# A decode-attention kernel with a gated MLP: other sizes and fewer pieces of K_0, V_15 and the output projection, and wq issued as 16 partitions and then 112

## The chip, the cores and the metric

The kernel runs on one core of one Trainium2 chip. The metric is the device time of one execution in microseconds (us), lower is better. A run is one execution; medians are over several runs. The span of a profile is a little shorter than the time of its run (650.4 against 652.2 us here), so spans are compared with spans and times with times.

## The reference

One token (S = 1, D = 512) goes through attention over a cache of 16384 keys in 32 heads of 128, and through a small gated MLP; a scalar gate mixes the two. All inputs are bf16.

```python
def _A_ref(x, k_cache, v_cache, wq, wo):                  # k_cache, v_cache: (1, 32, 16384, 128)
    q = (x @ wq).reshape(B, Sq, H, Dh).transpose(0, 2, 1, 3)   # wq: (512, 4096)
    scores = jnp.einsum('bhqd,bhkd->bhqk', q, k_cache) * Dh ** (-0.5)
    p = softmax(scores, axis=-1)
    o = jnp.einsum('bhqk,bhkd->bhqd', p, v_cache)
    return o.transpose(0, 2, 1, 3).reshape(B, Sq, H * Dh) @ wo  # wo: (4096, 512)

g = sigmoid((x * gate_w).sum(-1, keepdims=True))
return g * _A_ref(x, ...) + (1 - g) * _B_ref(x, ...)      # _B_ref: gated MLP, F = 1792  [cut]
```

The caches are 268 MB of the 279.6 MB read. Almost nothing is written.

## The kernel before

The heads are taken in 16 pairs. The keys of a pair (K_i) and its values (V_i) are 8 MB each, 128 partitions by 64 KB, and are loaded through three buffers of 8 MB in turn. A load waits, on the SyncE (SP) queue that issues it, until the load three places earlier has been used. The buffer that will hold V_0 first holds wq (4 MB), w_in and w_out.

```python
K_CUTS = (0, 128, 256)            # pieces of K_0 and K_15, of 256
V_CUTS = (0, 160, 224, 256)       # pieces of V_15; 32 of them are one tile on TensorE
WO_CUTS = (0, 16, 24, 28, 30, 31, 32)   # pieces of wo, in heads
WIDE = 24                         # heads taken in "wide" groups of 8; the rest one by one
...
sp.op(lambda e: e.dma_start(out=wq, in_=A_wq.rearrange("(p c) n -> p (c n)", c=DC)),
      inc=(ld_q, 16))
sp.op(... w_in ...); sp.op(... w_out ...)
...
for n, kind, i in loads:          # K_0, K_1, V_0, K_2, V_1, ...
    wait = [user[n - 3]] if n >= 3 else [w_free] if buf[n % 3] is setup else []
    ...
    if n == 0:
        cuts, sems = K_CUTS, ld_kf
    elif i == NP - 1:
        cuts, sems = (K_CUTS, ld_kh) if kind == "k" else (V_CUTS, ld_vp)
    ...
for j, (a, b) in enumerate(zip(WO_CUTS[:-1], WO_CUTS[1:])):
    sp.op(... wo[:, a * D:b * D] ..., inc=(ld_o[j], 16))
...
def add(lhsT, rhs, wait, mark=False):     # one head: two matmuls 1 x 256
    ...
for j, (a, b) in enumerate(zip(WO_CUTS[:-1], WO_CUTS[1:])):
    for k in range(max(a, WIDE), b):
        y_ok = add(o2[:, k:k + 1], wo[:, k * D:(k + 1) * D],
                   [(ld_o[j], 16)] if k == a else (), k == H - 1)
    if b == 28:
        add(ones_f[:, 0:1], d_sb[:, :], [w_ok])   # sum of the wide groups, copied by ScalarE
...
for q in (sp, act):
    open_late(nc, q)     # the first load of SP and of ScalarE is issued ahead of the start barrier
```

`k_s` and `v_s`, which tell VectorE (DVE) and TensorE (PE) that data is there, are raised by GpSimd when a load has landed.

The softmax here doesn't subtract the row's maximum and nothing guards it: scores larger than these inputs give would overflow.

## Time and profile before

| | before |
|---|---|
| time, median of the first 6 runs | 651.86 us (651.61 to 652.16) |
| span of the profile | 650.4 us |
| read from memory | 279.58 MB |
| first large DMA packet | 1.0 us |
| wq landed | 12.06 us |
| last load landed | 647.94 us |
| PE's last matmul ended | 648.80 us |

A landing is the time at which a load's data is complete. The landings are read from the trace's records of DMA packets (a packet is one piece that one of the 16 DMA engines moves): each load ends in sixteen semaphore writes of 4 bytes (720 for the 45 loads on the SP queue before), and the last of them is taken.

From the page (the summary that is kept of each profiled execution), the DMA rows (busy tenths of the 16 DMA engines in 40 slices of 16.3 us, and what they moved), the totals, and the row of wq in the table of DMA issues (KB, us from issue to landing):

```profile
span 650.4 us, 7753 instructions
...
DMA  9999999999998999999999999999999999999998
GB/s 382 444 439 451 447 391 451 451 431 407 451 451 387 451 451 447 391 451 451 407 431 451 447 391 451 451 431 407 451 451 395 443 451 447 391 439 463 394 427 341
...
HBM read 279.58 MB, written 0.00 MB: 430 GB/s over the span
...
bufs<-in_A_wq_dram SPq DMA_DIRECT2D x1, 4096.0 KB, 12.4
```

The kernel is bound by DMA from end to end. (The swing between 387 and 451 is only in which slice a long packet is counted. Sixteen packets are in flight at a time, and one of 64 KB takes 2.42 us: spread over their durations, the packets give 433 GB/s all the way.) At that rate 279.58 MB take 645.7 us, so a change can save at most the few microseconds at both ends.

The stretch in which wq arrives, in the view of windows (busy us and number of instructions for each engine, PE clock, DMA share, GB/s):

```profile
core 0: us, PE busy (x) PEld busy (x) DVE busy (x) ACT busy (x) POOL busy (x), PEclk, DMA share, GB/s
1.00:12.00 11.00, 0.61 (x4) 0.34 (x4) 4.56 (x5) 3.04 (x3) 1.95 (x6) 1.00 0.99 399
```

The end of the chain of work that ended last (start us, us, what). L101 are matmuls of the wide groups, L88 repeated matmuls (fillers, there to keep PE busy), L693 the heads taken one by one and the sum of the wide groups:

```profile
643.48 1.01 PE ps_all L101 x8
644.49 0.43 PE ps_all L88
644.92 0.85 PE ps_all L101 x6
645.77 0.43 PE ps_all L88
646.20 0.85 PE ps_all L101 x8
647.05 0.23 PE ps_all L88
647.28 0.42 PE ps_all L693 x8
647.70 0.02 issue
647.73 1.08 PE ps_all L693 x12
648.80 0.02 issue
648.83 0.41 DVE res L708
```

PE ends 0.86 us after the last landing (648.80 and 647.94), so PE and DMA end almost together.

And from the timeline, V_15's copy by ScalarE (ACT) out of PSUM, where PE's results (ps_all) stand; that is the end of V_15's work on PE:

```profile
639.29 0.59 ACT L578 COPY d_sb<-ps_all 128x512 f32<-128x512 f32 x1 [11.74 <-ACTq L84]
```

### The profile page before, as it was taken

To read this page: it belongs to the slowest core of one execution; us is meant where nothing else is said; L and a number is where in the kernel's file an instruction comes from. 1 tells how busy PE (TensorE), PEld (TensorE's weight loads), DVE (VectorE), ACT (ScalarE), POOL (GpSimd) and SP (SyncE) were. 2 spreads that over 40 slices of the span, in tenths; PEclk is the share of its full clock that TensorE was granted. 3 is DMA by queue.
4 is the path that set the end of the run, shared out by engine and by line. 5 is a ranking of instruction groups with operands and counts; after the bars stand their busy time and mean duration, and the time that the engine had idled before them with its cause. 6 is when DMAs were issued, how large, how long until landed. Compare 5 with 4: busy or idle time off the path is not lost. (4 is left out here: it accounts for less than half of the span.)

```text
span 650.4 us, 7753 instructions
## 1 busy us (share of the span) xinstructions
PE 437.8 (67%) x2462; PEld 46.9 (7%) x1320; DVE 336.4 (52%) x159; ACT 45.8 (7%) x112; POOL 2.2 (0%) x10
## 2 busy tenths in 40 slices
PE   0675876847477675857757486584858857488878
PEld 0000010000101000010100101000010100001022
DVE  3487719256280745618156370835628174465600
ACT  2211010100001000010100001000010100001011
POOL 1000000000000000000000000000000000000000
PEclk9868797958889687888958779795887969689888
DMA  9999999999998999999999999999999999999998
GB/s 382 444 439 451 447 391 451 451 431 407 451 451 387 451 451 447 391 451 451 407 431 451 447 391 451 451 431 407 451 451 395 443 451 447 391 439 463 394 427 341
DMA packets 6491, 279.60 MB, mean 430 GB/s; under 512 B 727, under 2 KB 986, under 8 KB 1370
## 3 DMA queue, kind: packets, MB, share of 16 engines
q1 hardware_dynamic: 6482, 279.58, 99.6%
q8 instruction: 1, 0.02, 0.0%
q10 hardware_dynamic: 8, 0.00, 0.0%
HBM read 279.58 MB, written 0.00 MB: 430 GB/s over the span
## 5 line engine op out<-in xcount | busy, mean ns | idle before, releaser
L557 DVE TENSOR_TENSOR bufs<-bufs,qb x64 | 281.5, 4419 | 165.1 <-DVEq L84 165.1
L88 PE MATMUL ps_all<-bufs,ident 128*128 x960 | 272.2, 444 | 0.0
L475 PE MATMUL ps_all<-bufs,ident 128*128 x64 | 28.8, 451 | 143.6 <-PEq L84 143.6
L101 PE MATMUL ps_all<-bufs,p_t 128*8 x1024 | 80.3, 388 | 28.9 <-PEq L84 18.3
L542 DVE TENSOR_REDUCE s_sb<-ps_all 128x64 f32<-128x512 f32 x64 | 44.1, 689 | 100.2 <-DVEq L84 100.2
L88 PE MATMUL ps_all<-zero,ident 128*8 128x512 bf16 (+1 forms) x147 | 57.3, 390 | 0.0
L569 ACT ACTIVATE p_t<-s_sb 64x256 f32 (+1 forms) x32 | 13.3, 415 | 439.7 <-ACTq L84 439.3
L475 PEld LDWEIGHTS ps_all<-bufs,ident 128*128 128x128 bf16 x64 | 6.3, 99 | 367.7 <-issue 367.7
L101 PEld LDWEIGHTS ps_all<-bufs,p_t 128*8 x1024 | 18.4, 82 | 162.3 <-issue 161.5
L510 PE MATMUL ps_all<-pick,d_sb 128*128 128x2 f32 x128 | 17.0, 254 | 14.8 <-PEq L84 14.8
L510 PEld LDWEIGHTS ps_all<-pick,d_sb 128*128 128x128 f32 x128 | 15.7, 193 | 22.9 <-issue 22.9
L578 ACT COPY d_sb<-ps_all 128x512 f32<-128x512 f32 x16 | 9.4, 586 | 103.5 <-ACTq L84 103.5
L583 ACT CAST ps_all<-zero 128x512 f32<-128x512 bf16 x15 | 8.8, 589 | 1.7
L458 PE MATMUL ps_all<-zero,ident 128*128 128x512 bf16 x18 | 7.0, 389 | 0.0
L364 DVE TENSOR_TENSOR bufs<-ps_all,ident 128x896 f32<-128x896 f32 x2 | 2.1, 1086 | 8.3 <-PE ps_all L88 8.3
L647 DVE TENSOR_TENSOR o_sb<-ps_all,rl 128x32 bf16<-128x32 f32 x1 | 0.2, 192 | 11.4 <-PE ps_all L510 11.4
L306 PE MATMUL ps_all<-xgw,const-float32-1.0 1*128 1x3 f32 x2 | 0.6, 360 | 8.0 <-DVE xgw L303 8.0
L569 ACT ACTIVATION_READ_ACCUMULATOR p_t<-s_sb (+1 forms) x32 | 5.9, 185 | 0.0
L644 DVE RECIPROCAL rl<-ps_all 128x32 f32<-128x32 f32 x1 | 0.4, 358 | 10.4 <-PE ps_all L531 10.4
L88 PE MATMUL ps_all<-bufs,xb 128*128 x12 | 4.9, 536 | 0.0
L101 PE MATMUL ps_all<-bufs,u 128*1 x14 | 2.6, 372 | 3.1 <-ACT ps_all L410 2.4
L329 PE MATMUL ps_all<-bufs,xb 128*128 x4 | 2.3, 573 | 3.2 <-DMA bufs<-in_B_w_in_dram 3.2
(76 smaller groups left out, 44.9 us busy)
## 6 DMA issues: line engine op xcount, KB each, us to landing
bufs<-in_A_k_cache_dram SPq DMA_DIRECT2D x4, 4096.0 KB, 33.7
bufs<-in_A_v_cache_dram SPq DMA_DIRECT2D x1, 5120.0 KB, 33.1
bufs<-in_A_wq_dram SPq DMA_DIRECT2D x1, 4096.0 KB, 12.4
bufs<-in_A_v_cache_dram SPq DMA_DIRECT2D x1, 2048.0 KB, 37.6
bufs<-in_A_wo_dram SPq DMA_DIRECT2D x1, 2048.0 KB, 23.6
bufs<-in_B_w_in_dram SPq DMA_DIRECT2D x1, 1792.0 KB, 15.6
bufs<-in_A_v_cache_dram SPq DMA_DIRECT2D x1, 1024.0 KB, 39.6
bufs<-in_A_wo_dram SPq DMA_DIRECT2D x1, 1024.0 KB, 25.7
```

The source lines that it names most:

```text
L88: ins = eng.matmul(out, lhsT=lhsT, rhs=rhs, **flags).ins
L101: ins = eng.matmul(bank[0:m, 0:n], lhsT=lhsT, rhs=rhs, **flags).ins
L329: if n else matmul_on(nc, e, lambda: e.matmul(args[0], lhsT=args[1], rhs=args[2], **flags), [at, (xa, 0)]))
L364: dve.op(lambda e, h=h, zh=zh: e.tensor_tensor(out=zm[:, 2 * h * ZB:2 * (h + 1) * ZB].rearrange("p (b m k) -> p b m k", b=2, k=FhC), in0=z ...
L458: e.matmul(args[0], lhsT=args[1], rhs=args[2], **flags)
L475: matmul_on(nc, e, lambda: e.matmul(s3, lhsT=ident[:, :], rhs=k3[:, :, 0:W], start=True, **flags), [(kw, 0)])
L510: ins = e.matmul(o2, lhsT=d_sb[:, r * Dh:(r + 1) * Dh], rhs=pick[:, r * 2:(r + 1) * 2], start=False, stop=False, skip_group_check=True)
L542: return e.tensor_reduce(out=s_sb[:, c * QK:(c + 1) * QK], in_=s_ps[c % 2].rearrange("p (j w) -> p j w", w=W), axis=AX.X, op=ALU.add)
L557: e.tensor_tensor(out=k3, in0=k3, in1=qi, op=ALU.mult).then_inc(mul_s, 1)
L569: e.activation(out=p_t[rows, bass.ds(at, NG * 8)].rearrange("p (t c) -> p t c", c=8)[:, :, 4 * s:4 * s + 4], in_=s_sb[rows, :].rearrange(" ...
L578: return e.copy(out=d_sb[:, :], in_=d_ps)
L583: e.copy(out=d_ps, in_=zero[:, :]).then_inc(drn_s, 1)
```

## The change

Its intent, as far as the edit shows it, is fewer loads and an earlier first packet: the first load has 16 rows, one for each of the 16 DMA engines, and both loads of wq are issued ahead of the start barrier. The end on PE is cut to fit: two wide groups, and the sum of the wide groups is added first.

```diff
--- before.py
+++ after.py
@@ -36,9 +36,9 @@
 NT = NG // TG
 ZB = F // 4
 K_CUTS = (0, 128, 256)
-V_CUTS = (0, 160, 224, 256)
-WO_CUTS = (0, 16, 24, 28, 30, 31, 32)
-WIDE = 24
+V_CUTS = (0, 192, 256)
+WO_CUTS = (0, 16, 27, 31, 32)
+WIDE = 16
 inv_sqrt_dh = float(Dh) ** -0.5
 
 
@@ -151,7 +151,7 @@
             todo.append(i)
 
 
-def open_late(nc, queue):
+def open_late(nc, queue, loads):
     kind = queue.eng.engine
     blocks = {b.name: b for b in nc.m.functions[0].blocks}
     first = nc.m.functions[0].blocks[0].instructions
@@ -159,10 +159,11 @@
     barrier = [i for i in first[at:] if i.engine == kind][:2]
     assert isinstance(barrier[1], mybir.InstEventSemaphore)
     todo = blocks[queue.name].instructions
-    assert isinstance(todo[0], mybir.InstDMACopy)
     for i in barrier:
         first.remove(i)
-    todo[1:1] = barrier
+    n = next(j for j, i in enumerate(todo) if not isinstance(i, mybir.InstDMACopy))
+    assert n >= loads
+    todo[loads:loads] = barrier
 
 
 def gated_mix_kernel(nc, A_x, A_k_cache, A_v_cache, A_wq, A_wo, B_x, B_w_in, B_w_sp, B_b_sp,
@@ -233,7 +234,6 @@
         sem(n) for n in ("ld_x", "ld_g", "ld_q", "ld_w", "ld_u", "st_out"))
     ld_k = [sem(f"ld_k{b}") for b in range(2)]
     ld_v = [sem(f"ld_v{b}") for b in range(2)]
-    ld_kf = [sem(f"ld_kf{b}") for b in range(len(K_CUTS) - 1)]
     ld_kh = [sem(f"ld_kh{b}") for b in range(len(K_CUTS) - 1)]
     ld_vp = [sem(f"ld_vp{b}") for b in range(len(V_CUTS) - 1)]
     ld_o = [sem(f"ld_o{b}") for b in range(len(WO_CUTS) - 1)]
@@ -273,8 +273,9 @@
     act.op(lambda e: e.dma_start(out=wb_row[:, 0:1], in_=B_w_sp), inc=(ld_g, 16))
     act.op(lambda e: e.dma_start(out=wb_row[:, 1:2], in_=B_b_sp.rearrange("(a d) -> a d", a=1)),
            inc=(ld_g, 16))
-    sp.op(lambda e: e.dma_start(out=wq, in_=A_wq.rearrange("(p c) n -> p (c n)", c=DC)),
-          inc=(ld_q, 16))
+    wq_src = A_wq.rearrange("(p c) n -> p (c n)", c=DC)
+    for a, b in ((0, 16), (16, P)):
+        sp.op(lambda e, a=a, b=b: e.dma_start(out=wq[a:b], in_=wq_src[a:b]), inc=(ld_q, 16))
     sp.op(lambda e: e.dma_start(out=w_in, in_=B_w_in.rearrange("(p c) f -> p (c f)", c=DC)),
           inc=(ld_w, 16))
     sp.op(lambda e: e.dma_start(out=w_out, in_=B_w_out.rearrange("(p k) n -> p (k n)", k=FhC)),
@@ -338,7 +339,7 @@
     z_ok = (pe.sem, pe.n)
     def pe_queries(e):
         e.wait_ge(*g_free)
-        e.wait_ge(ld_q, 16)
+        e.wait_ge(ld_q, 32)
         wq4 = wq.rearrange("p (c n j s d) -> p c n j s d", c=DC, n=4, s=2, d=Dh)
         xa, wa = (counter(e, n, 0) for n in ("xq", "wq"))
         with e.Fori(0, DC) as c:
@@ -608,9 +609,7 @@
         wait = [user[n - 3]] if n >= 3 else [w_free] if buf[n % 3] is setup else []
         src = (k_src if kind == "k" else v_src)[i]
         cuts, sems = (0, KP), [(ld_k if kind == "k" else ld_v)[i % 2]]
-        if n == 0:
-            cuts, sems = K_CUTS, ld_kf
-        elif i == NP - 1:
+        if i == NP - 1:
             cuts, sems = (K_CUTS, ld_kh) if kind == "k" else (V_CUTS, ld_vp)
         for a, b, done in zip(cuts[:-1], cuts[1:], sems):
             sp.op(lambda e, a=a, b=b, n=n, src=src: e.dma_start(
@@ -626,8 +625,7 @@
         e.nop().then_inc(loaded, -16)
 
     def pool_pairs(e):
-        for j in range(len(ld_kf)):
-            hand(e, ld_kf[j], k_s, 1)
+        hand(e, ld_k[0], k_s, 2)
         with e.Fori(0, NP // 2 - 1):
             hand(e, ld_k[1], k_s, 2)
             hand(e, ld_v[0], v_s, NT)
@@ -696,12 +694,11 @@
                 mark=mark and s == NC - 1, inc=(half, 1) if mark and s == 0 else None)
         return ok
 
+    add(ones_f[:, 0:1], d_sb[:, :], [w_ok])
     for j, (a, b) in enumerate(zip(WO_CUTS[:-1], WO_CUTS[1:])):
         for k in range(max(a, WIDE), b):
             y_ok = add(o2[:, k:k + 1], wo[:, k * D:(k + 1) * D],
                        [(ld_o[j], 16)] if k == a else (), k == H - 1)
-        if b == 28:
-            add(ones_f[:, 0:1], d_sb[:, :], [w_ok])
     for q in (dve, act):
         mine = range(NC)[:NC // 2] if q is dve else range(NC)[NC // 2:]
         for s in mine:
@@ -722,8 +719,8 @@
     for q in (sp, pool, act, dve, pe):
         q.issue()
     nc.switch_bb("end")
-    for q in (sp, act):
-        open_late(nc, q)
+    open_late(nc, sp, 2)
+    open_late(nc, act, 1)
 
 
 _INS = ['A_x', 'A_k_cache', 'A_v_cache', 'A_wq', 'A_wo', 'B_x', 'B_w_in', 'B_w_sp', 'B_b_sp', 'B_w_out', 'gate_w']
```

The order of instructions on the engines is otherwise that of before.

## The prediction

> **What bounds the kernel now.** DMA. In the page's 40 slices DMA is busy at nine tenths or more nearly everywhere; 279.58 MB pass in 650.4 us. In the trace's packet records the first large packet starts 1.0 us after the span's start, each engine then moves 32 KB packets back to back in 1.21 us (16 engines: 432 GB/s), and the last load lands at 647.9 us. 279.58 MB at 433 GB/s is 645.7 us: only some 5 us are not streaming, at the start and after the last landing. PE (67%) and DVE (52%) have slack; the DMA issues show 30 to 40 us from issue to landing, so the queue never runs dry.
>
> **The change, part by part.**
>
> 1. K_0 in one piece. By the timeline DVE starts on K_0 at 32.7 us, on its first half; the whole lands at 37.8. DVE starts some 5.5 us later, and K_0's buffer comes free at about 67 instead of 61.1 us. The next load need only be queued before V_0 has landed, at 76.5 us. Nothing on the critical path.
>
> 2. Fewer pieces. Near the end 1 KB packets take 46 ns where 38 would be full rate; a small piece costs about 0.07 us. Three net fewer: -0.2 to -0.3 us.
>
> 3. Tail (timeline from 615 us). PE takes V_15 as 5, 2, 1 tiles, from 631.15 us, 0.6 us after the landing. With 6 and 2 it starts at about 633.6. A tile costs 0.93 us at full clock, 1.28 in the half-clock window seen from 630 to 637 us. So V_15 ends about 641.9 instead of 639.0, and the chain to the output projection moves with it. Then two wide groups instead of three, but PE waits for ACT's 0.59 us copy right after them, and 16 narrow heads at 0.15 us follow instead of 8. PE, no longer the last landing, ends the kernel: about +3 us.
>
> 4. wq as 16 and 112 partitions. Meant to start the first packets sooner; worth at most 0.3 us. [...]
>
> **Prediction.** 651.9 + 3.0 + 2.4 - 0.3 = 657.0 us; 8 in 10 between 653.3 and 662.5. Faster by over 2%: 0.005; within 2%: 0.925; slower by over 2%: 0.07.
>
> **What would show it.** First 16 packets of wq at 2 to 5 us, and wq landing later than 12.1 us: step 4 right. If later ones stay at 1.21 us and wq lands at 12, step 4 is about -0.3 and the time near 654.5. The last load landing while PE is still in V_15 or the wide groups, and a final chain of PE alone: step 3 right. DVE's first multiply near 38 us plus step 4's delay, no DMA gap near 76 us: step 1 right.
>
> **What would make it wrong.** The 112 rows spread so badly that wq takes 20 us more (slower by over 2%)[...].

The sum came to 657.0 us: +3.0 for the tail (step 3), +2.4 for wq (step 4) and -0.3. The +2.4 was the estimate that packets into 16 and into 112 partitions would be slow; the ground given for it is cut, as no trace had shown it, and so is one case of what would make the forecast wrong. The "at most 0.3 us" of step 4 is an estimate too: before, the sixteen first packets start from 1.00 to 1.75 us, at 1.26 us on average.

## The result, and the profile after

| | before | after |
|---|---|---|
| time, median | 651.9 us (20 runs, 651.61 to 652.84) | 662.15 us (10 runs, 660.94 to 663.03) |
| ratio of fast runs | | 1.0156, 95% interval 1.0147 to 1.0165 |
| span of the profile | 650.4 us | 660.6 us |
| wq landed | 12.06 us | 20.64 us |
| last load landed | 647.94 us | 657.04 us |
| PE's last matmul ended | 648.80 us | 659.00 us |

A ratio is the mean time of one kernel's fast runs over that of the other's of the same rounds, so it is not quite the ratio of the medians quoted. By the threshold of 2% the two are "the same"; the difference of 10 us is nonetheless far outside the noise.

The rows of the page that answer to those above:

```profile
span 660.6 us, 7753 instructions
...
DMA  9999999999999999999999999999999999999997
GB/s 222 389 444 436 440 393 444 444 440 436 425 413 444 444 436 440 421 417 444 444 436 433 405 440 444 444 433 436 405 440 444 444 433 433 405 438 450 426 413 306
...
HBM read 279.58 MB, written 0.00 MB: 423 GB/s over the span
...
bufs<-in_A_wq_dram SPq DMA_DIRECT2D x1, 3584.0 KB, 21.3
...
bufs<-in_A_wq_dram SPq DMA_DIRECT2D x1, 512.0 KB, 6.5
```

The first slice moves 222 instead of 382 GB/s, although its DMA digit is still a 9: the engines are busy, with packets that take longer. The windows say the same of the stretch in which wq arrives (it is 19.6 us long now):

```profile
core 0: us, PE busy (x) PEld busy (x) DVE busy (x) ACT busy (x) POOL busy (x), PEclk, DMA share, GB/s
1.00:20.60 19.60, 0.61 (x4) 0.35 (x4) 4.56 (x5) 3.04 (x3) 1.95 (x6) 1.00 1.01 226
```

The end of the chain of work that ended last, and V_15's copy in the timeline (L691 are now the single heads and the sum, L101 the second wide group):

```profile
655.32 0.63 PE ps_all L101 x8
655.95 0.02 issue
655.97 0.59 ACT d_sb L687
656.56 0.04 issue
656.61 2.39 PE ps_all L691 x36
659.00 0.02 issue
659.02 0.41 DVE res L705
```

```profile
650.82 0.58 ACT L579 COPY d_sb<-ps_all 128x512 f32<-128x512 f32 x1 [14.00 <-ACTq L84]
```

So there are two losses. The stream is late by 8.6 us when wq has landed and by 9.1 us at its end, and PE ends 1.96 us instead of 0.86 us after the last landing, another 1.1 us.

The packet records show the first loss in detail. All rows of wq are 32 KB. Sorted by start, sixteen at a time (one per engine), they took on average, in us:

| packets | before | after |
|---|---|---|
| 1 to 16 | 1.89 | 3.62 |
| 17 to 32 | 1.24 | 2.80 |
| 33 to 48 | 1.22 | 2.29 |
| 49 to 64 | 1.21 | 1.79 |
| 65 to 80 | 1.21 | 1.80 |
| 81 to 96 | 1.21 | 2.04 |
| 97 to 112 | 1.21 | 2.27 |
| 113 to 128 | 1.21 | 2.10 |

All 16 engines take part in both kernels: at 3 us sixteen packets are in flight in both traces. 112 rows are seven groups of sixteen packets. The engines do start a little sooner (1.00 to 1.38 us after the change, 1.00 to 1.75 us before), as intended. All later loads run at 1.21 us for 32 KB and 2.42 us for 64 KB, as before.

### The profile page after: what moved, and what is told of

Same layout as the page of the kernel before. It is cut to its first block, busy times and chain, and to the rows that moved or that the text cites. A ratio compares the mean times of both kernels' runs of the same rounds, so it can differ in the third digit from the quotient of the medians.

```text
span 660.6 us, 7753 instructions
## 1 busy us (share of the span) xinstructions
PE 431.5 (65%) x2469; PEld 47.6 (7%) x1328; DVE 336.3 (51%) x159; ACT 45.8 (7%) x112; POOL 2.1 (0%) x10
## 5 line engine op out<-in xcount | busy, mean ns | idle before, releaser
L88 PE MATMUL ps_all<-bufs,ident 128*128 x960 | 267.5, 436 | 0.0
L476 PE MATMUL ps_all<-bufs,ident 128*128 x64 | 28.6, 447 | 148.0 <-PEq L84 148.0
L101 PE MATMUL ps_all<-bufs,p_t 128*8 x1024 | 80.4, 389 | 31.7 <-PEq L84 21.1
L101 PEld LDWEIGHTS ps_all<-bufs,p_t 128*8 x1024 | 18.5, 82 | 164.8 <-issue 164.0
L330 PE MATMUL ps_all<-bufs,xb 128*128 x4 | 2.1, 517 | 4.0 <-DMA bufs<-in_B_w_in_dram 4.0
```

The source lines that it names most:

```text
L88: ins = eng.matmul(out, lhsT=lhsT, rhs=rhs, **flags).ins
L101: ins = eng.matmul(bank[0:m, 0:n], lhsT=lhsT, rhs=rhs, **flags).ins
L330: if n else matmul_on(nc, e, lambda: e.matmul(args[0], lhsT=args[1], rhs=args[2], **flags), [at, (xa, 0)]))
L476: matmul_on(nc, e, lambda: e.matmul(s3, lhsT=ident[:, :], rhs=k3[:, :, 0:W], start=True, **flags), [(kw, 0)])
```

## The experiments

Main theory, at the start: the cost lies in the destination. The packets of a load that covers only some of the partitions of SBUF (the on-chip memory that the loads fill) last longer because of the partitions that they go to, as the first sixteen do after the change (3.62 us against 1.89). The expectations call this the "port theory". Rivals: a second load or the later barrier costs the time; the memory side does (rows read in another order); only odd sizes such as 112 are slow. For the other parts of the change: they cost about 1 us on PE (from the traces), or 2.7 us (the prediction), and K_0 nothing. Twelve kernels were run, four or five runs and one profile of each; each was also checked against the reference.

### 1. wq alone in 16 and 112 partitions

```diff
 kernel before, plus:
-sp.op(... out=wq, in_=A_wq ...)
+for a, b in ((0, 16), (16, P)):
+    sp.op(... out=wq[a:b], in_=wq_src[a:b] ...)
+open_late(nc, sp, 2)
```

> The kernel before with wq alone issued as 16 and 112 partitions (both ahead of the start barrier, as in the change). Port theory: the whole loss at the start comes back, +8.6 to +9.1 us (ratio 1.013 to 1.014), the first 16 packets last 3 to 4 us, wq lands near 20.6 us instead of 12.1. Rival, that the late start of everything else or another part of the change costs the time: under +1 us, wq lands by 12.5 us.

Measured: 661.27 us against 651.77, ratio 1.0144 (1.0128 to 1.0159), that is +9.4 us. wq landed at 20.74 us, and its packets took 3.56, 2.81, 2.26, 1.82, 1.77, 2.03, 2.25 and 2.09 us, the pattern of the changed kernel. This part alone makes over nine tenths of the loss.

### 2. wq in two loads cut by columns

```diff
 kernel before, plus:
+for a, b in ((0, 2048), (2048, DC * HDh)):
+    sp.op(... out=wq[:, a:b], in_=wq_src[:, a:b] ...)
+open_late(nc, sp, 2)
```

> The kernel before with wq also in two loads, both ahead of the start barrier, but cut by columns: 2048 of the 16384 elements of all 128 partitions, then the rest. Port theory: every partition range stays whole, so within 0.3 us of before (ratio 0.9995 to 1.0005). Rival, that a second load or the later barrier costs the time: +8 to +9 us as with the rows.

Measured: 651.75 us against 651.77, ratio 0.9997 (0.9982 to 1.0013). Windows of this kernel, while wq arrives (columns as before):

```profile
1.00:12.00 11.00, 0.61 (x4) 0.34 (x4) 5.57 (x8) 3.04 (x3) 1.95 (x6) 1.00 1.01 406
```

The number of loads, the sizes (0.5 and 3.5 MB) and the barrier are those of experiment 1. Only the direction of the cut differs, and the loss is gone. The second load and the barrier are not the cause.

### 3. The changed kernel with wq whole

```diff
 kernel after, plus:
-for a, b in ((0, 16), (16, P)): ...
+sp.op(... out=wq, in_=A_wq ...)
-open_late(nc, sp, 2)
+open_late(nc, sp, 1)
```

> The changed kernel with wq in one load again. From the two traces (last landing +9.1 us, end +10.2 us) the rest of the change should cost +1.1 us (ratio 1.0017); the prediction on record had +2.7 us for it (3.0 - 0.3, ratio 1.004). If the parts are not additive, anything else.

Measured: 652.63 us against 651.77, ratio 1.0015 (0.9999 to 1.0030), four runs of 652.32, 654.10, 652.94 and 651.67 us. By the ratio that is +1.0 us, near the +1.1 expected, but the interval just holds zero, and the profiled run's span was 650.4 us, no longer than before. The parts are additive within the noise: 9.4 + 1.0 is 10.4, and 10.2 was measured.

### 4. K_0 in one load

```diff
 kernel before, plus:
-if n == 0:
-    cuts, sems = K_CUTS, ld_kf
+# K_0 is loaded and handed over whole
```

> The kernel before with K_0 in one load. Theory: DVE starts 5 to 6 us later but the loads never wait, so 0 us (-0.2 to +0.2, ratio within 0.0004 of 1). Rival, that the late start is carried through the pairs to the end: +5 us (1.008).

Measured: 651.88 us against 651.77, ratio 0.9999 (0.9986 to 1.0013). DVE's first multiply on K_0, from the timeline of before and of this kernel:

```profile
32.73 4.43 DVE L557 TENSOR_TENSOR bufs<-bufs,qb  x1 [0.42 <-DVEq L84]
```

```profile
38.35 4.42 DVE L556 TENSOR_TENSOR bufs<-bufs,qb  x1 [6.13 <-DVEq L84]
```

The start is 5.6 us later and costs nothing that the times can show: the next loads stand 30 to 40 us in the queue before they land.

### 5. wq in two halves

```diff
 kernel of experiment 1, but:
-for a, b in ((0, 16), (16, P)):
+for a, b in ((0, 64), (64, P)):
```

> The kernel before with wq as partitions 0 to 63 and 64 to 127. Port theory[...], 2.4 us a packet, wq lands near 20.5 us, time +8 to +10 us, although no piece is odd in size. Rival, that only the odd 112 or the small 16 is slow: within 0.5 us of before.

Measured: 662.29 us against 651.80, ratio 1.0160 (1.0143 to 1.0177), +10.4 us. The seven groups of sixteen packets after the first took 2.41 to 2.56 us each, about twice 1.21, and wq landed at 22.02 us. Windows of this kernel, columns as before:

```profile
1.00:21.00 20.00, 0.58 (x4) 0.34 (x4) 5.60 (x8) 3.04 (x3) 1.95 (x6) 1.00 1.00 211
```

So an even cut costs as much as the odd one: sixteen packets of 32 KB in 2.55 us are 206 GB/s, where 1.21 us are 433. The trace shows each half at half rate, as estimated (2.4 us a packet, twice 1.21).

### 6 to 8. The same 16 rows into partitions 0 to 15, every fourth, every seventh

Each of these loads the first 16 rows of wq once more, ahead of wq, into a buffer that is free at that time; K_1's load then waits for that. Only the destination differs between the three.

```diff
 kernel before, plus, ahead of wq's load:
+sp.op(... out=buf[1][0:16, 0:16384], in_=wq_src[0:16] ...)        # extra_low16
+sp.op(... out=buf[1][0:64:4, 0:16384], in_=wq_src[0:16] ...)      # extra_step4
+sp.op(... out=buf[1][0:112:7, 0:16384], in_=wq_src[0:16] ...)     # extra_step7
```

> The kernel before with one extra load ahead of wq: the first 16 rows of wq (0.5 MB) into partitions 0 to 15 of a buffer that is free then. The bytes alone are worth +1.2 us. Port theory[...]: first 16 packets of 3 to 4 us as in the changed kernel, time +2.9 to +3.9 us. Rival, that the source rows or the 16-row shape cause it (memory side): the same 3 to 4 us, and then also in the two runs beside it.

> As extra_low16, same source rows and bytes, but into partitions 0, 4, 8 to 60[...]. First packets of 2.2 to 2.8 us, time between the other two, +1.3 to +2.4 us. Memory-side rival: the same as extra_low16.

> As extra_low16, same source rows and bytes, but into partitions 0, 7, 14 to 105[...]. First packets near the 1.9 us of the kernel before, time +1.0 to +1.7 us, the bytes alone. Memory-side rival: the same as extra_low16, +2.9 us or more.

The packet times expected of the last two are estimates; the ground given for them is cut. 2.2 to 2.8 us lies between the 1.89 us of the kernel before and the 3.62 us of the changed one, and 1.9 us is that of the kernel before.

Measured:

| | partitions 0 to 15 | every 4th | every 7th |
|---|---|---|---|
| first 16 packets, mean | 3.65 us | 2.13 us | 1.70 us |
| idle engine time before their next packet, summed over 16 engines | 0.2 us | 2.8 us | 13.4 us |
| wq landed | 15.72 us | 16.47 us | 15.79 us |
| time, against 651.80 us | 655.77 | 655.67 | 655.57 |
| ratio | 1.0059 (1.0042 to 1.0075) | 1.0056 (1.0040 to 1.0073) | 1.0061 (1.0044 to 1.0078) |

The packets came in the order expected (2.13 us is just under the 2.2 to 2.8 expected), and the source was the same in all three, so the destination decides how long a packet takes. There is one profile of each, but the first sixteen packets took 3.56 to 3.65 us in the profiles of all four kernels that begin with 16 rows into partitions 0 to 15, and 1.87 to 1.92 us in those of before and of experiments 3 and 4, where wq is whole. The times did not follow: all three medians are +3.8 to +4.0 us, where +1.0 to +2.4 was expected of the last two. Taken alone the times fit the memory-side rival, which expected the same of all three; its packets of 3 to 4 us in all three did not come. The packet records show the reason only in part. In those two, engines that were done early stood idle, for wq's first packets on them started as late as 5.3 us (every 4th) and 5.4 us (every 7th); wq is issued behind the barrier here, at 1.3 us in the timelines. Why some of its packets start 4 us after the issue is open. And the time follows the last engine, not the mean: with every 4th, twelve of the sixteen engines had finished wq by 13.94 us and one only at 16.47, and at the end of the stream they were still 2.4 us apart (649.93 to 652.35; before 0.6, from 647.38 to 647.94). These times are therefore no clean price of the destination; the packet durations are a better one.

### 9. The 112 rows read from elsewhere

```diff
 kernel of experiment 1, but (the result is wrong on purpose for the queries):
-in_=wq_src[a:b]
+in_=wq_src[a:b] if a == 0 else k_src[0][a:b, 0:DC * HDh]
```

> wq_rows with its 112 rows read from the first key pair instead, where rows are 64 KB apart and not 32 KB; the destination is the same, the result is wrong on purpose. Destination-side theory: the packets of the 112 rows keep their pattern (about 2.8, 2.3, 1.8, 1.8, 2.0, 2.25, 2.1 us) and the time stays +9 to +10 us. Memory-side rival: another pattern, packets nearer 1.2 us, +2 to +5 us.

Measured: 661.20 us against 652.00, ratio 1.0144 (1.0128 to 1.0159). The packets took 3.65, 2.83, 2.28, 1.86, 1.80, 2.03, 2.26 and 2.12 us, within 3% of experiment 1 in each group. With another row pitch in memory the same pattern stays, so the memory-side rival falls for the 112 rows too. (The check of the output, at its tolerance, let this result pass although its queries are wrong; it is no proof of anything here.)

### 10 and 11. V_15 alone, and the output projection alone

```diff
 kernel before, plus (v_two):
-V_CUTS = (0, 160, 224, 256)
+V_CUTS = (0, 192, 256)
 kernel before, plus (wo_four):
-WO_CUTS = (0, 16, 24, 28, 30, 31, 32); WIDE = 24
+WO_CUTS = (0, 16, 27, 31, 32); WIDE = 16
+add(ones_f[:, 0:1], d_sb[:, :], [w_ok])    # ahead of the single heads, not after head 27
```

> The kernel before with V_15 alone in two pieces of 6 and 2 tiles (192 and 64 of 256). Theory: PE starts V_15 some 2.4 us later, ends it 1.2 to 2.4 us later, and with the three wide groups still to come PE and not the last landing ends the kernel: +0.8 to +1.8 us (ratio 1.0012 to 1.0028), as much as the kernel with both tail changes (+1.0). Rival, that the shift is swallowed by the waits for the output weights: 0.

> The kernel before with the output projection alone changed (pieces of 16, 11, 4, 1 heads, two wide groups, the sum of the wide groups added first). Theory: with V_15 done as early as before, PE still waits for the last landing, so 0 us (-0.2 to +0.2). The prediction's account of the tail (16 narrow heads and a wait for ACT) would make PE the last: +0.5 to +1 us.

Measured: v_two 652.30 us against 652.00, ratio 1.0006 (0.9992 to 1.0019); wo_four 652.19 us, ratio 1.0004 (0.9991 to 1.0018). Neither is clear of zero. v_two came out below the range expected, though its interval (-0.5 to +1.2 us) reaches into it; wo_four's (-0.6 to +1.2 us) holds both the 0 of the theory and the +0.5 to +1 of the prediction's account. In the one profile of each, PE's last matmul ended 1.88 us (v_two) and 1.25 us (wo_four) after the last landing, against 0.86 us before and 1.96 us after the change. v_two's trace points the way of the theory; wo_four's, 0.4 us later than before, lies between the two accounts. The times cannot decide at this size.

### 12. The two parts that might help

```diff
 kernel before, plus experiment 2 (wq by columns) and experiment 4 (K_0 whole)
```

> The two parts of the change that can help, without the rest: K_0 in one load, and wq in two loads cut by columns, on the kernel before. The last landing should come 0.4 to 0.5 us earlier; the end follows only as far as PE lets it: -0.1 to -0.5 us (ratio 0.9992 to 0.9999).

Measured: 652.02 us against 652.00, ratio 0.9998 (0.9984 to 1.0012); no gain shown. In its profile one or a few engines fell behind by over 1 us at some 95 us: seven packets of 64 KB that started from 95.07 to 97.67 us took 2.60 to 4.33 us where 2.42 is usual, and from then on the sixteen engines ended a load 1.6 us apart instead of 0.45, up to 643.8 us. The lag was not made up, and the last landing came at 648.87 us, later than before and not earlier. No experiment points to a version that beats the kernel before.

## Why the prediction was right, and where its sizes were off

The range of 653.3 to 662.5 us held the 662.15 us measured, barely: the sum had foreseen +5.1 us, half of the loss of 10.2. Both losses came where the sum had put them, at wq and in the tail; two terms of the sum were mis-sized, in opposite directions. That the result fell inside was partly luck: had the tail cost the +3 that it was given, and not +1, the time would have been about 664 us.

- **What bounds the kernel: right.** The stream runs at 433 GB/s in both, and nearly everything that delayed it at the start is still there at the end (8.6 us at wq's landing, 9.1 us at the last one).
- **Step 4, wq: right in kind, mis-sized.** The sum had +2.4 us; experiment 1 measured +9.4. Nothing in the traces of the time supported that size, which was the author's estimate. The first 16 packets took 4.1 us from first start to last end, 128 GB/s (122 to 125 in experiments 1, 6 and 9). The 112 took 15.5 us after that (5.1 to 20.6), 237 GB/s, where 8.5 us would be the 433 GB/s of the stream. Shown: the cost goes with the direction of the cut (+9.4 us by rows in experiment 1, ratio 0.9997 by columns in 2), not with odd size (+10.4 us for halves, 5), number of loads (2) or the row pitch of the source (661.20 us, 9), and the packets' duration follows the destination's partitions (3.65, 2.13 and 1.70 us, 6 to 8). Not shown: what it is about these partitions that makes packets slow, and why all engines slow down alike in the 112 rows (1.79 to 2.80 us a group).
- **The first packets sooner, at most 0.3 us: right** in kind. The last engine started at 1.38 instead of 1.75 us. It is lost in what follows.
- **Step 3, the tail: right in kind, too large.** +3 was predicted, the traces show +1.1 us and experiment 3 +1.0 (its interval holds zero). V_15's end moved by 650.82 - 639.29 - 9.1 = 2.4 us, near the 2.9 predicted. But before, the wide groups waited for wo's first piece (landed 642.82 us, wide groups from 643.48), while after the change that piece had landed at 652.05 us, over 2 us before. The first group began at 654.40 us by the timeline, which is 654.40 - 643.48 - 9.1 = 1.8 us later. And before, the wide groups ran in a half-clock stretch, after the change at full clock: one took 0.92 us there against some 1.28 before. From the first wide group to PE's last matmul it is 4.60 instead of 5.32 us. So of the 2.4 us 0.6 went into the wait that was there before and 0.7 into a shorter end, and 1.1 is left. How much of the 0.7 is the clock and how much the other make-up of the end was not separated. The prediction had used the right durations for a tile, but had carried the whole shift of V_15 to the end, without the wait and with the clock as before.

The clock in the windows of before (first two lines) and after (last two), column PEclk:

```profile
636.80:643.40 6.60, 5.21 (x44) 2.08 (x35) 0.60 (x3) 1.18 (x2) 0.00 (x0) 1.00 1.00 425
643.60:646.90 3.30, 3.30 (x27) 0.45 (x16) 0.00 (x0) 0.00 (x0) 0.00 (x0) 0.50 0.98 393
```

```profile
638.20:648.30 10.10, 5.80 (x51) 1.88 (x48) 0.60 (x2) 0.00 (x0) 0.00 (x0) 0.50 0.92 394
648.50:660.00 11.50, 9.03 (x95) 3.91 (x84) 1.01 (x4) 2.12 (x4) 0.00 (x0) 1.00 0.67 278
```

By the traces' clock records the half-clock stretches of both kernels last multiples of 3.41 us (3.41 to 13.65 us before, 3.41 to 20.48 after), and they fall differently in the ends of the two kernels (the last full one begins at 643.54 us before and at 638.12 us after). Whether that causes the wider spread of the changed end (651.67 to 654.10 us in experiment 3) was not tested.

- **Step 2, fewer pieces, -0.2 to -0.3 us: not shown.** The last landing of experiment 3 came 0.4 us before that of the kernel before (647.53 and 647.94), but of that 0.1 us was there when wq had landed, and experiment 12 shows that one execution can differ by more.
- **Step 1, K_0: right.** Its cost is zero within 0.14% (experiment 4). In the changed kernel DVE's first multiply came at 47.84 us by the timeline, near the 38 us plus the delay of step 4, and the DMA moved 450 GB/s from 70 to 100 us, without a gap.

## What to carry to other kernels

In a DMA-bound kernel, cut a load by columns and keep all 128 partitions in every piece: two loads cut by columns cost nothing here, while the same bytes cut by partitions, 16 and 112 or 64 and 64, ran at about half rate (226 and 211 GB/s while wq arrived, against 399) and delayed everything behind them by 9 to 10 us. Read DMA by packet durations and GB/s and not by busy share, which was 0.99 while wq arrived before the change and 1.01 after it, at 399 and 226 GB/s. A stage that is not the bottleneck may be movable at no cost (here the start on K_0, by 5.6 us), and at the end of the kernel a shift on one engine is partly swallowed by a wait that was there before. Look at the last of the DMA engines and not at their mean: a lag of one or a few engines stayed to the end of the stream in experiment 7 (2.4 us) and nearly so in 12 (1.6 us).
